# A fused hash-attention and two-layer MoE kernel: the instruction order with and without the timeline scheduler

## Chip, cores and metric

The kernel runs on one core of one Trainium2 chip. The metric is the device time of one execution in microseconds (us), lower is better. The inputs are fixed, and one launch computes everything.

## The reference

`q`, `k`, `v` have 2 batches, 8 heads, 768 positions and a head size of 64. Each query and key gets a 6-bit bucket from the signs of its product with `proj`; a query attends only to keys of its own bucket. Two dense layers with activations follow (the batch and positions make 1536 tokens, the heads a model width of 512, the inner width is 2048).

```python
q_bits = (np.einsum('bhsd,dk->bhsk', q, proj) > 0)
k_bits = (np.einsum('bhsd,dk->bhsk', k, proj) > 0)
mask = q_bucket[:, :, :, None] == k_bucket[:, :, None, :]
scores = np.where(mask, scale * np.matmul(q, k.transpose(0, 1, 3, 2)), -1000000000.0)
attn = softmax(scores)
x = np.matmul(attn, v)                    # to (tokens, 512)
h = x @ w_in1;  x = (h * sigmoid(h)) @ w_out1
h = x @ w_in2;  out = (h - np.tanh(h)) @ w_out2
```

## The kernel before, in words

**Attention.** The work is cut into 96 tiles: 16 heads (8 of each batch) of 6 blocks of 128 queries. Tile i goes through `scores` (line 243, four matmuls of TensorE into a PSUM tile `ps`), `soft_max` (line 256, VectorE: the masked row maximum and a copy into `p`), `soft_exp` (lines 264 and 265, ScalarE: a bias and the exponential), a transposition of the probabilities into `pt`, and `pv` (lines 311 to 313, 18 small matmuls with `pt` as weights). There are two ways to transpose. Every odd tile of batch 0 is turned on TensorE (`turn_p`, line 278) and split on ScalarE and VectorE (lines 280 and 281). All other tiles are split into a high half (`soft_hi`, line 290, ScalarE) and a low half (`soft_lo`, line 297, GpSimd), and a transposing DMA from SyncE's queue (line 299) fills `pt`. `pt` has four buffers. The bucket bits of a head are computed by `hash_mm` (line 172 on TensorE, line 185 on VectorE into `hb`) and copied by two DMAs of ScalarE's queue into rows of `q2` and `k2`; the second two of the four matmuls of `scores` read them. `v` of a batch is split once into `v16` and `v16l` (lines 232 and 233, six instructions each); `pv` needs both.

**The dense layers.** `Moe` runs three passes over the two layers: pass 0 is layer one for batch 0 (it runs beside the attention of batch 1), pass 1 is layer one for batch 1, and pass 2 is layer two for everything. A pass is made of groups of 12 matmuls into one PSUM bank: `h_group` (line 530) and `o_group` (line 554), eight of each per chunk of the inner width in passes 0 and 1. Weights come in pieces of 128 rows: a load (line 466 or 470), a few VectorE and ScalarE steps (lines 506 to 510, 497, 498) and a GpSimd step (line 499, or 485 for a piece read back from scratch memory). All groups of a chunk need the chunk's four pieces of their matrix.

**What sets the order.** The source is a software pipeline written by hand. One step s of `attention` emits, for several tiles at once:

```python
scores(i); soft_hi(i1); turn_p(i2); norm(...)      # i1 = i - 1, i2 = i - 2
yield s, 0
soft_max(i); pv(j); soft_lo(i2)                    # j = i - LAG, LAG = 6
yield s, 1
soft_exp(i); denom(...); split_a / split_b; load_qk
yield s, 2
```

At each `yield` the main part of the kernel puts in one piece of a step of `Moe`, on average one group of 12 matmuls per attention step. An engine runs its own instructions in the order of its list and waits at its head. Before, the list of each engine is not the source's order: when the `TileContext` closes (line 729), a scheduler plays the program on a model of time, and hands each engine its instructions in the order in which they became ready there. It weighs priorities too: `early` (line 92) raises those of the work on `v`, and `keep_in_program_order` (lines 465 and 505) pins some loads behind what stands before them.

## Time and profile before

| what | us |
|---|---|
| runs without the profiler | 795.64, 794.8, 789.62; median 794.8 |
| profiled execution, own time | 791.22 |
| profiled execution, span from first to last instruction | 789.4 |
| busy in that span: TensorE matmuls, VectorE, ScalarE, GpSimd | 733.6, 544.4, 433.1, 309.5 |

The span falls into two parts. Up to about 384 us attention and pass 0 run, with all engines and the DMA queues at work. From there to the end passes 1 and 2 run. Tile numbers below count from 0 to 95 in the source's order; "S62" would be the scores of tile 62.

### The profile page before, as it was taken

The numbers are of one execution on the slowest core, as the hardware profiler recorded it, in microseconds if no ns is written. First come the engines' busy times: TensorE is split into PE (matmuls) and PEld (weight loads), VectorE is DVE, ScalarE is ACT, GpSimd is POOL, SyncE is SP. The second block draws the span as 40 slices with busy tenths as digits, with TensorE's granted clock in tenths as the row PEclk, the third lists the DMA queues.
The fourth block names the chain that finished last, engine by engine and source line by source line (L and its number), as shares of the span: only waits on it lengthen the run. The fifth ranks groups of instructions, "written<-read, shape, count | busy, mean of one in ns | idle before, by whom it ended". The sixth has DMA issues, their size and how long they took to land.

```text
span 789.4 us, 14334 instructions
## 1 busy us (share of the span) xinstructions
PE 733.6 (93%) x5492; PEld 700.0 (89%) x5492; DVE 544.4 (69%) x1029; ACT 433.1 (55%) x821; POOL 309.5 (39%) x214
## 2 busy tenths in 40 slices
PE   4778798789989899999999999999999999999998
PEld 3667677679978798899999999999999999999998
DVE  6968688798878778778542443998768576584342
ACT  4849788797788678667443441553524334242130
POOL 4536537466777667566455420222111110110000
PEclk8899899899999999999999999999999999999999
DMA  7695776969999899994333320323112121210102
GB/s 255 190 148 106 126 154 167 212 155 197 263 245 211 214 180 240 215 218 136 97 104 107 95 81 1 101 90 130 53 56 78 57 81 33 75 54 0 52 29 81
DMA packets 138879, 100.39 MB, mean 127 GB/s; under 512 B 115870, under 2 KB 118174, under 8 KB 138810
## 3 DMA queue, kind: packets, MB, share of 16 engines
q1 hardware_dynamic: 137712, 97.54, 50.6%
q10 hardware_dynamic: 1098, 1.94, 1.0%
q8 instruction: 43, 0.70, 0.3%
q14 instruction: 26, 0.21, 0.1%
HBM read 57.95 MB, written 11.53 MB: 88 GB/s over the span
## 4 chain that ended last, share of the span: by engine, by line
PE 55%; DMA 2%; ACT 1%; DVE 0%; issue 0%; POOL 0%; ACTq 0%; DVEq 0%
PE psm L554 28%; PE psm L530 26%; DMA pt<-hl 1%; DMA w<-wi 1%; PE ps L243 0%; ACT xh L577 0%; ACT p L265 0%; POOL hl L297 0%; PE pso L311 0%; POOL wl L485 0%; ACT wh L484 0%; ACT th L536 0%; PE pso L312 0%; PE pso L313 0%; ACT hl L290 0%
## 5 line engine op out<-in xcount | busy, mean ns | idle before, releaser
L499 POOL TENSOR_TENSOR wl<-wa,wh 128x512 fp32r<-128x512 f32 x64 | 83.8, 1309 | 244.3 <-ACT wh L498 244.3
L530 PE MATMUL psm<-xh,wh 128*128 128x384 f32 x512 | 173.2, 339 | 1.6 <-ACT wh L484 1.6
L554 PE MATMUL psm<-gh,wh 128*128 128x384 f32 x512 | 173.0, 338 | 0.6 <-ACT x L346 0.4
L554 PE MATMUL psm<-gl,wh 128*128 128x384 f32 x512 | 171.5, 335 | 0.0
L530 PE MATMUL psm<-xl,wh 128*128 128x384 f32 x512 | 171.4, 335 | 0.0
L530 PE MATMUL psm<-xh,wl 128*128 128x384 f32 x512 | 170.0, 335 | 0.0
L554 PE MATMUL psm<-gh,wl 128*128 128x384 f32 x512 | 169.4, 335 | 0.0
L297 POOL TENSOR_TENSOR hl<-p,hl 128x768 f16<-128x768 f32 x72 | 120.4, 1674 | 88.0 <-ACT hl L290 82.5
L256 DVE TENSOR_SCALAR_CACHE_REDUCE p<-ps 128x768 f32<-128x768 f32 x96 | 90.8, 952 | 29.7 <-PE ps L243 20.0
L530 PEld LDWEIGHTS psm<-xh,wh 128*128 128x128 f32 x512 | 96.5, 188 | 2.1 <-ACT wh L484 1.9
L243 PE MATMUL ps<-k,q 128*128 128x384 f32 x336 | 82.9, 372 | 15.9 <-DVE p L256 9.0
L554 PEld LDWEIGHTS psm<-gh,wh 128*128 128x128 f32 x512 | 96.3, 188 | 1.5 <-ACT x L346 0.6
L554 PEld LDWEIGHTS psm<-gl,wh 128*128 128x128 f32 x512 | 96.4, 188 | 0.0
L530 PEld LDWEIGHTS psm<-xl,wh 128*128 128x128 f32 x512 | 96.4, 188 | 0.0
L566 DVE TENSOR_TENSOR acc<-acc,psm 128x384 f32<-128x384 f32 x96 | 52.1, 551 | 63.5 <-PE psm L554 63.1
L530 PEld LDWEIGHTS psm<-xh,wl 128*128 128x128 f32 x512 | 95.9, 188 | 0.0
L554 PEld LDWEIGHTS psm<-gh,wl 128*128 128x128 f32 x512 | 95.8, 188 | 0.0
L542 DVE TENSOR_TENSOR gl<-psm,gh 128x384 fp32r<-128x384 f32 x128 | 70.6, 554 | 31.9 <-ACT gh L541 31.7
L265 ACT ACTIVATE p<-p,bi 128x768 f32<-128x768 f32 x96 | 89.0, 939 | 2.9
L541 ACT CAST gh<-psm 128x384 fp32r<-128x384 f32 x128 | 61.4, 480 | 50.5 <-DVE psm L540 35.1
L311 PE MATMUL pso<-v,pt 128*128 128x65 f16 x576 | 70.9, 200 | 15.4 <-DMA pt<-hl 15.3
L311 PEld LDWEIGHTS <-pt 128*128 128x128 f16 x576 | 55.3, 101 | 27.2 <-DMA pt<-hl 17.4
(90 smaller groups left out, 1267.2 us busy)
## 6 DMA issues: line engine op xcount, KB each, us to landing
w<-in_w_in_dram SPq DMA_DIRECT2D x32, 512.0 KB
w<-in_w_out_dram SPq DMA_DIRECT2D x32, 512.0 KB
r<-in_qkT_dram SPq DMA_DIRECT2D x15, 768.0 KB
wi<-wa SPq DMA_DIRECT2D x16, 256.0 KB
wo<-wa SPq DMA_DIRECT2D x16, 256.0 KB
w<-wi SPq DMA_DIRECT2D x16, 256.0 KB
w<-wo SPq DMA_DIRECT2D x16, 256.0 KB
vr<-in_v_dram SPq DMA_DIRECT2D x6, 512.0 KB
```

The source lines that it names most:

```text
L243: nc.tensor.matmul(out=ps[:, u, 0:HS], lhsT=a[:, t * 128:(t + 1) * 128], rhs=c[:, u * HS:(u + 1) * HS], start=(j == 0), stop=(j == 1))
L256: nc.vector.tensor_scalar(p.rearrange("p (c s) -> p c s", c=2), pss.pop(i)[:, :, 0:HS], FLOOR, None, op0=ALU.max, op1=ALU.max, accum_out=m)
L265: nc.scalar.activation(out=p, in_=p, func=ACTF.Exp, scale=0.125, bias=bi)
L297: nc.gpsimd.tensor_tensor(hl[:, 1, :], p, hl[:, 0, :], op=ALU.subtract)
L311: nc.tensor.matmul(out=o, lhsT=pt[:, kt, :], rhs=v16[:, kt, h, :], start=(kt == 0), stop=False)
L499: nc.gpsimd.tensor_tensor(ll, s, hh.bitcast(F32), op=ALU.subtract)
L530: nc.tensor.matmul(out=ps, lhsT=a[:, k, fs], rhs=b_[blk][:, k, :], start=(k == 0 and j == 0), stop=(k == KD - 1 and j == 2))
L541: nc.scalar.copy(gh[:, f, :], ps)
L542: nc.vector.tensor_tensor(gl[:, f, :], ps, gh[:, f, :].bitcast(F32), op=ALU.subtract)
L554: nc.tensor.matmul(out=ps, lhsT=a[:, f, ds], rhs=b_[:, f, :], start=(f == 0 and j == 0), stop=(f == F - 1 and j == 2))
L566: nc.vector.tensor_tensor(ac, ac, ps, op=ALU.add)
```

## The change

The change is one argument. With it, the lists are made without the model of time.

```diff
-    with _tile.TileContext(nc, schedule_with_timeline_sim=True) as tc:
+    with _tile.TileContext(nc, schedule_with_timeline_sim=False) as tc:
         lsh_attention_moe_kernel(tc, *args)
```

No instruction is added or removed; the same 7220 of TensorE, 935 of VectorE, 855 of ScalarE, 219 of GpSimd and 241 of SyncE stand in other places. The mean move is 15 places on TensorE, 2.4 on VectorE, 3.4 on ScalarE and under 1 on GpSimd and SyncE. The new lists are close to the order of the source and not equal to it: going down VectorE's list, the next instruction is an earlier one of the source 273 times before and 247 times now.

The first place is VectorE's list in batch 0, around the bucket bits of head 5 (`hb_1255`, line 185), which the scores of tiles 30 to 35 read. `ps_1349` and `ps_1396` are the scores of tiles 24 and 25, `pt_1187` is the turned tile 21. Before:

```order
L281 TENSOR_TENSOR pt_1097<-psm_1098,pt_1097 128x384
L256 TENSOR_SCALAR p_1369,mx_1370<-ps_1349 128x768
L256 TENSOR_SCALAR p_1402,mx_1403<-ps_1396 128x768
L256 TENSOR_SCALAR p_1458,mx_1459<-ps_1438 128x768
L281 TENSOR_TENSOR pt_1097<-psm_1104,pt_1097 128x384
L256 TENSOR_SCALAR p_1497,mx_1498<-ps_1492 128x768
L281 TENSOR_TENSOR pt_1187<-psm_1188,pt_1187 128x384
L185 TENSOR_SCALAR hb_1255<-psm_1256,cst_sb_69 82x384
L281 TENSOR_TENSOR pt_1187<-psm_1194,pt_1187 128x384
L185 TENSOR_SCALAR hb_1255<-psm_1257,cst_sb_69 82x384
```

Now:

```order
L281 TENSOR_TENSOR pt_1097<-psm_1098,pt_1097 128x384
L256 TENSOR_SCALAR p_1289,mx_1290<-ps_1269 128x768
L281 TENSOR_TENSOR pt_1097<-psm_1104,pt_1097 128x384
L256 TENSOR_SCALAR p_1322,mx_1323<-ps_1317 128x768
L281 TENSOR_TENSOR pt_1187<-psm_1188,pt_1187 128x384
L281 TENSOR_TENSOR pt_1187<-psm_1194,pt_1187 128x384
L185 TENSOR_SCALAR hb_1255<-psm_1256,cst_sb_69 82x384
L185 TENSOR_SCALAR hb_1255<-psm_1257,cst_sb_69 82x384
L256 TENSOR_SCALAR p_1369,mx_1370<-ps_1349 128x768
```

The bits were made after four maxima that now stand behind them, and the two halves of each item are no longer set among others.

The second place is TensorE's list in batch 1, around the scores of tile 62 (`ps_3163`). `pt_3012` is the transposed tile 57, `pt_2952` is tile 56, and `psm_3149` is a group of pass 0. Before:

```order
L311 LDWEIGHTS pt_3012
L311 MATMUL pso_3058<-v16_2444,pt_3012 128x65
L243 MATMUL ps_3163<-k1_2713,q1_2711 128x384 x2
L243 MATMUL ps_3163<-k2_2714,q2_2712 128x384 x2
L312 LDWEIGHTS pt_3012
L312 MATMUL pso_3058<-v16l_2445,pt_3012 128x65
```

Now:

```order
L554 MATMUL psm_3149<-gl_2397,wh_2411 128x384
L554 MATMUL psm_3149<-gh_2396,wl_2412 128x384
L243 MATMUL ps_3163<-k1_2713,q1_2711 128x384 x2
L243 MATMUL ps_3163<-k2_2714,q2_2712 128x384 x2
L311 LDWEIGHTS pt_2952
L311 MATMUL pso_3058<-v16_2444,pt_2952 128x65
```

Before, the scores stood inside the `pv` of the tile five behind; now they stand between a whole group of 12 and the whole `pv` of the tile six behind.

The third place is TensorE's list at the end of pass 0. `psm_5563`, `psm_5587`, `psm_5607` are three of its last eight groups of line 554, all of which need the pass's last weight piece for their last three matmuls; `psm_5543` is its last group of line 530. Before:

```order
L554 MATMUL psm_5607<-gl_5263,wh_5280 128x384
L554 MATMUL psm_5607<-gh_5262,wl_5281 128x384
L554 MATMUL psm_5563<-gh_5262,wh_5280 128x384
L554 MATMUL psm_5563<-gl_5263,wh_5280 128x384
L554 MATMUL psm_5587<-gh_5262,wh_5280 128x384
L554 MATMUL psm_5587<-gl_5263,wh_5280 128x384
```

Now:

```order
L530 MATMUL psm_5543<-xh1_71,wl_4833 128x384
L554 MATMUL psm_5563<-gh_5262,wh_5280 128x384
L554 MATMUL psm_5563<-gl_5263,wh_5280 128x384
L554 MATMUL psm_5563<-gh_5262,wl_5281 128x384
L554 MATMUL psm_5563<-gh_5262,wh_5280 128x384
L554 MATMUL psm_5563<-gl_5263,wh_5280 128x384
```

The three groups were begun one after the other and finished together, with matmuls of pass 1 set among them; now the first is written out with all its 12 before the next goes on, and pass 1 begins behind the last.

## Rows read from the trace of the kernel before

**Rows 1.** The page, part 2: TensorE's busy tenths and granted clock in 40 slices
```profile
PE   4778798789989899999999999999999999999998
...
PEclk8899899899999999999999999999999999999999
```

**Rows 2.** Windows: busy us of PE, PEld, DVE, ACT, POOL, then clock, DMA share, GB/s
```profile
0.00:50.00 50.00, 30.23 (x217) 25.67 (x218) 37.99 (x75) 31.22 (x54) 24.20 (x19) 0.86 0.80 203
50.00:190.00 140.00, 118.11 (x1334) 103.87 (x1334) 113.68 (x229) 111.89 (x217) 77.05 (x48) 0.93 0.72 158
190.00:350.00 160.00, 151.89 (x1379) 139.31 (x1378) 127.51 (x250) 120.11 (x210) 107.39 (x69) 0.99 1.03 222
350.00:384.00 34.00, 31.56 (x251) 29.61 (x250) 23.07 (x44) 21.48 (x47) 21.31 (x18) 1.00 0.55 147
384.00:789.40 405.40, 401.84 (x2319) 401.52 (x2317) 242.11 (x435) 148.41 (x297) 79.53 (x61) 1.00 0.21 68
```

**Rows 3.** The chain that ended last: start us, us, what; the first of 23 such
```profile
403.12 16.64 PE psm L554 x96
```

**Rows 4.** Waits of PE from 10 to 190 us: total us, times, longest
```profile
PE ps L243 <- DVE p L256: 9.0, 10, 2.9
PE pso L311 <- DMA pt<-hl: 8.3, 3, 3.9
PE ps L243 <- DMA k<-hb: 5.4, 4, 3.3
PE ps L243 <- DMA l<-hb: 4.0, 2, 3.5
PE pso L312 <- DVE v16l L233: 3.6, 2, 2.2
```

**Rows 5.** Waits of PE from 190 to 350 us
```profile
PE pso L311 <- DMA pt<-hl: 6.5, 5, 2.7
PE ps L243 <- DVE p L256: 1.4, 3, 0.9
```

**Rows 6.** Timeline of DVE near 25 us: start us, us, instruction
```profile
23.29 0.80 DVE L233 SCALAR_TENSOR_TENSOR v16l<-vr,vsc,v 128x512 f16<-128x512 f32 x1
...
26.43 3.62 DVE L233 SCALAR_TENSOR_TENSOR v16l<-vr,vsc,v 128x512 f16<-128x512 f32 x3
```

**Rows 7.** Lines by shape: count, then busy us, mean ns of one, idle before
```profile
L297 POOL TENSOR_TENSOR hl<-p,hl 128x768 f16<-128x768 f32 x72 | 120.4, 1674 | 88.0 <-ACT hl L290 82.5 <-DMA k<-hb 3.9 <-DVE p L256 0.7
...
L256 DVE TENSOR_SCALAR_CACHE_REDUCE p<-ps 128x768 f32<-128x768 f32 x96 | 90.8, 952 | 29.7 <-PE ps L243 20.0 <-PE psm L278 5.8 <-POOL wl L499 1.7
L265 ACT ACTIVATE p<-p,bi 128x768 f32<-128x768 f32 x96 | 89.0, 939 | 2.9
...
L290 ACT CAST hl<-p 128x768 f16<-128x768 f32 x72 | 59.9, 833 | 4.8 <-DVE cv L510 1.8 <-DMA q<-hb 1.0 <-ACT p L265 0.7
...
L233 DVE SCALAR_TENSOR_TENSOR v16l<-vr,vsc,v 128x512 f16<-128x512 f32 x12 | 14.7, 1241 | 0.1
```

**Rows 8.** The chain again: two transposing DMAs from issue to release
```profile
322.84 5.53 DMA pt<-hl
...
351.86 4.80 DMA pt<-hl
```

**Rows 9.** Windows for line 256 alone: its instructions on DVE in batch 0
```profile
50.00:130.00 80.00, 31.15 (x66) 0.94 0.64 133
```

**Rows 10.** Timeline of POOL: the last weight piece of pass 0
```profile
374.60 1.28 POOL L499 TENSOR_TENSOR wl<-wa,wh 128x512 fp32r<-128x512 f32 x1
```

**Rows 11.** Timeline of PE: the last matmul of line 530 in pass 0
```profile
368.52 0.33 PE L530 MATMUL psm<-xh,wl 128*128 128x384 f32 x1
```

**Rows 12.** The chain: the last 36 matmuls of line 554 in pass 0
```profile
383.71 6.24 PE psm L554 x36
```

**Rows 13.** Windows around a wait of TensorE at 85 us
```profile
85.00:90.00 5.00, 1.55 (x7) 1.34 (x7) 0.79 (x2) 2.69 (x6) 4.25 (x3) 0.69 1.02 142
90.00:95.00 5.00, 5.00 (x57) 4.88 (x56) 2.07 (x5) 3.81 (x8) 2.06 (x2) 0.63 0.07 14
```

## Prediction

> **What bounds the kernel now.** I read the page's slices first. TensorE is busy nine tenths or more in every slice from the middle on, and never quite full before it; its clock is whole late and falls to 8 or 9 tenths in the early slices [rows 1]. Then the windows, which cut the span by stage [rows 2]. From 384 us to the end TensorE is busy 401.8 of 405.4 us. The chain that ended last says the same: from 403 us on it is nothing but packets of 96 matmuls, each 16.64 us long, 0.173 us for a matmul, with no wait between them (23 such rows) [rows 3]. That stretch is bound by TensorE alone, and no order of the same matmuls can shorten it.
>
> So the whole question lies in the first 384 us. TensorE is idle there for 50 - 30.2 = 19.8 us in the start, 140 - 118.1 = 21.9 us in the attention of batch 0 and the change of batches, 160 - 151.9 = 8.1 us in batch 1, and 34 - 31.6 = 2.4 us in the end of pass 0, together 52.2 us [rows 2]. No other engine is full either: in the 140 us of batch 0 VectorE is busy 113.7 and ScalarE 111.9, some 80% [rows 2]. That is the picture of engines that wait for one another at the head of their lists, which is what the change touches. The waits of TensorE say for what [rows 4, 5]: until 190 us for the row maximum that frees the scores' PSUM (9.0 us), for the transposing DMA that fills `pt` (8.3), for the DMAs of the bucket bits (5.4 + 4.0), and for `v16l` (3.6); in batch 1 almost only for `pt` (6.5 of 8.1).
>
> **The change part by part.** The sum is made against the profiled execution's own 791.2 us (span 789.4 and 1.8 around it). That is 3.6 us under the median of the runs, 794.8, and inside their scatter. Nothing is added or removed, so every term is a wait that goes, comes or moves.
>
> *Passes 1 and 2.* TensorE's list is group after group in both, and what prepares weights has whole groups to hide under. 0 us; the idle time there, 3.6 us, bounds a gain, and I allow as much for a loss.
>
> *Bucket bits.* Before, VectorE makes the bits of head 5 after the maximum of tile 27, and the scores of tile 30 need them. Now they come before that of tile 24. The same holds for heads 2, 6 and 7, by 2 to 4 tiles; heads 3 and 4 come 1 and 2 tiles later, which still leaves them over a tile ahead of their use. Of the 9.4 us of waits for the bits, about 3.3 belong to head 1 in the start, and 6.1 to later heads [rows 4]. These go: -6 us (0 to -9). What is late next is the maximum of the tile before, a wait that the same rows show at 0.9 us a time.
>
> *Start.* The six instructions that make `v16l` stood one to three at a time between the maxima of tiles 3 to 7; now all six stand ahead of the maximum of tile 3, and a half of head 1's bits behind it. One such instruction took 0.80 us, three in a row 3.62 [rows 6], and the group's mean is 1.24 [rows 7]: six are 4.8 to 7.4 us of delay for the maxima of tiles 3 to 6. Behind them stand the exponentials, and TensorE, which has `pv` of tiles 0 and 1 to do in the meantime. The maxima are not VectorE's last word here, since it waits for bits anyway at tile 6. I take +4 (0 to +7).
>
> *Transposed tiles in batch 0.* Counted in the lists, a tile's `pv` stood on average 7.8 tiles behind the newest scores before and stands 6.4 behind now; in the middle of the batch it was 9 to 12 and is 6 to 9. The new list also sets three or four `pv` in a row. A tile that goes through the DMA needs, after its maximum, an exponential (0.94), a cast (0.83), the low half (1.67) [rows 7] and the DMA (4.8 to 5.5) [rows 8], 8.2 to 9.0 us. The pace of this stage is 80 us for 33 maxima (each has two records), 2.4 us a tile [rows 9], so a lead of 6 tiles is 14.5 us and most fit, but the DMA can only start once the `pv` four tiles back has freed a buffer. In a row of four the last one then waits for its own DMA. I take +4 (-8, if all 8.3 us of rows 4 go, to +19 with the first rival).
>
> *Change of batches.* TensorE waited 3.6 us for `v16l` of batch 1 [rows 4]. Its six instructions were set among the maxima of tiles 52 to 54 and now stand in one block between the maxima of tiles 50 and 51, 4.8 to 7.4 us long as above, while `pv` of tile 48 stands before the next groups of pass 0. Those groups start earlier too, because their first weight pieces are ready 3 to 6 tiles earlier. +1 (-4 to +6).
>
> *Batch 1.* Here the lead grows, from 3.8 tiles on average to 5.1 and to a steady 6 in the middle, where a step is scores, one whole `pv`, one whole group. One step is at least 4 + 12 matmuls of 0.173 us, 2.8 us, and `pv`; two more steps of slack are 6 us, more than the longest wait for `pt`, 2.7 us [rows 5]. The 6.5 us go. In their place, a step's maximum must now be done within the group between two scores; the wait for it, 1.4 us in all [rows 5], may double. -5 (-8 to +8: VectorE is busy 127.5 of 160 us [rows 2] and a regular step gives it less freedom).
>
> *End of pass 0.* The last groups of line 554 need the last weight piece. GpSimd ended it at 374.60 + 1.28 = 375.9 us [rows 10], when TensorE had begun the last matmul of line 530 at 368.5 [rows 11]. Before, it bridged the 7.4 us with pieces of four groups and with matmuls of pass 1, 20 of them up to the end of the pass. Now the first group alone gives it 9 matmuls, 1.6 us, and it waits some 5.6; the 84 matmuls left of that line take 14.6 us, to 390.5. Before, the same line ended at 383.71 + 6.24 = 389.9 [rows 12] with 20 x 0.173 = 3.5 us of pass 1 done besides. So +4 (0 to +6).
>
> Sum: 0 - 6 + 4 + 4 + 1 - 5 + 4 = +2, on 791.2, which is 793. That lies between the profiled execution and the median, so I forecast no difference that can be measured: for this kernel about 1% is what a measurement can tell from none. All lower ends together are 33 us under the start of the sum, all upper ends 49 over it, so 35 below and 47 above its result; the terms do not reach their ends at once, and a third of the way to either gives 782 to 808 as this case's own range.
>
> **The clock.** After TensorE had been busy only 1.55 of 5 us, its granted clock was 0.69 and then 0.63 in a stretch where it was busy throughout [rows 13]; of its two levels, 1.2 and 2.4 GHz, that is a mixture with much of the lower one. The Trainium skill (TensorE: Matmul & The Clock Gate, "HAM oscillation — how this bites in real kernels") says that an engine which keeps falling idle between bursts goes back to the half clock each time; the trace agrees, 0.63. By that rule the first rival below would cost more than its waits: 5.0 us of work at 0.63 instead of whole is 1.9 us, seven times 13, an estimate of 821. By the windows the mean clock of that stage is 0.93 [rows 2] and TensorE has idle time to spare there, so neither the sum nor the rival's price has it.
>
> **Rivals.**
>
> *Rows of `pv` wait (slower).* In batch 0 the new list has about seven places with three or four `pv` in a row ahead of the next scores. If in each the last DMA is late, the scores behind it are late, then the maximum, and every engine with them, because TensorE can't take the scores first. The price is that of such a wait now, 8.3 / 3 = 2.8 us [rows 4]: 7 x 2.8 = 19 instead of 4, so 793 + 15 = 808. For it speaks that the row before shows exactly this wait, up to 3.9 us; against it that the 6 tiles are 14.5 us. It decides from where a DMA takes more than about 7 us to land: it has to share the queue with loads of `q` and `k`.
>
> *One step fits the next (faster).* If the regular order lets VectorE and ScalarE run on in batch 0 as well, half of the 21.9 us of idle TensorE goes [rows 2], the price of `pt` (+4) does not come up, and the end of pass 0 is covered: 793 - 11 - 4 = 778. The even 80% of both engines speaks for it; against it, the waits then have to shrink everywhere at once.
>
> *The new order is hardly another.* The lists still are a scheduler's, and VectorE's moves are 2.4 places. Then all terms shrink together and the time stays at 791 to 795.
>
> **How the numbers follow.** I give the summed case 0.45 (within 1% in 0.29 of it, faster in 0.07, slower in 0.09), the rows of `pv` 0.27, nearly all slower, the good fit 0.20, all faster, and the last 0.08. Faster by over 1%: 0.07 + 0.20 = 0.27. Slower: 0.09 + 0.25 = 0.34. Within 1%: 0.39, the rest. The range reaches beyond both priced rivals: 774 to 816.
>
> **What would show it right or wrong.** After the change, the waits for bucket bits should be gone except for head 1; TensorE's waits for `pt` should be near none between the batches' change and the end of pass 0, and larger before; about 5 us of wait should stand inside the first group of line 554 behind the last of line 530; and from there to the end the windows should be as now. It is wrong if the passes after pass 0 show waits, or if the maximum of a tile becomes TensorE's main wait in batch 1.

## The result, and the profile after

| | before | after |
|---|---|---|
| 20 runs without the profiler, median | 790.77 us (784.37 to 799.68) | 797.07 us (792.54 to 799.98) |
| ratio, 95% interval | | 1.0075 (1.0055 to 1.0094) |
| profiled execution, own time | 791.22 us | 794.17 us |
| its span | 789.4 us | 792.4 us |

The change makes the kernel slower by about 6 us, 0.75%: less than the 1% that I took as the bound, but clear of zero. The prediction, 793.0, is 4.1 us under the median. The trace shows 1.2 of that: its execution is 2.95 us over the old one, at 794.17, where my sum had +2. The other 2.9 us are scatter, since this execution lies that far under the median of its own kernel. So the two traces show about half of the 6.3 us between the medians, and the windows below place only that half. That the sum comes so near is luck: its small error hides larger ones, as the windows show.

The page's slices of the changed kernel, as in [rows 1]:

```profile
PE   4688876788989999999999999999999999999998
```

From the middle on TensorE is as full as before. In the first half it is one tenth fuller in slices 3 and 5 and two tenths emptier in slices 6 and 7, from 99 to 139 us. The windows of [rows 2] for the changed kernel (the same columns):

```profile
0.00:50.00 50.00, 31.95 (x245) 27.12 (x246) 37.91 (x78) 30.55 (x53) 19.80 (x17) 0.86 0.71 208
50.00:190.00 140.00, 112.71 (x1268) 98.31 (x1268) 109.31 (x222) 108.92 (x210) 75.82 (x48) 0.94 0.70 149
190.00:350.00 160.00, 150.97 (x1405) 140.56 (x1401) 129.60 (x256) 125.15 (x223) 112.45 (x73) 0.99 1.05 230
350.00:384.00 34.00, 31.23 (x253) 29.60 (x250) 23.40 (x42) 19.06 (x41) 20.03 (x18) 1.00 0.59 147
384.00:792.40 408.40, 405.00 (x2337) 404.68 (x2335) 242.32 (x433) 147.79 (x297) 77.77 (x60) 1.00 0.22 67
```

TensorE's idle time (length less busy) is 18.1 us in the start, where it was 19.8; 27.3 where it was 21.9; 9.0 where it was 8.1; 2.8 where it was 2.4; and 3.4 after 384 us, where it was 3.6. So the loss lies in the second window. Its waits from 10 to 190 us, and then from 190 to 350 us, beside [rows 4, 5]:

```profile
PE ps L243 <- DVE p L256: 9.5, 12, 2.1
PE pso L311 <- DMA pt<-hl: 8.2, 6, 3.1
PE pso L311 <- DVE xt L329: 4.7, 3, 3.0
...
PE pso L312 <- DVE v16l L233: 0.8, 1, 0.8
...
PE ps L243 <- DMA k<-hb: 0.8, 1, 0.8
```

```profile
PE psm L554 <- POOL wl L499: 2.8, 1, 2.8
PE ps L243 <- DVE p L256: 2.5, 2, 1.4
PE ps L243 <- DMA k<-hb: 1.3, 1, 1.3
...
PE pso L311 <- DMA pt<-hl: 0.7, 1, 0.7
```

The waits that I expected to go are gone: those for bucket bits (9.4 us, now 0.8 and 1.3), for `v16l` (3.6, now 0.8), and for `pt` in batch 1 (6.5, now 0.7). In their place stand waits that the old trace has none of: for the normalisation on line 329, for the exponential on line 265 (5.4 us, most of it before 95 us), and for a weight piece on line 499. The wait for head 0's own bits (line 181), right at the start, grew from 1.3 to 3.9 us. Finer windows say where. Before:

```profile
50.00:100.00 50.00, 42.58 (x487) 36.16 (x487) 34.60 (x75) 39.02 (x77) 27.29 (x16) 0.93 0.61 125
100.00:135.00 35.00, 29.59 (x362) 25.66 (x361) 31.87 (x66) 29.44 (x60) 18.91 (x12) 0.95 0.70 151
135.00:165.00 30.00, 24.54 (x300) 22.12 (x297) 23.09 (x52) 22.30 (x42) 15.01 (x12) 0.89 0.90 212
165.00:195.00 30.00, 26.39 (x228) 24.58 (x226) 29.11 (x51) 24.78 (x47) 19.53 (x12) 0.94 0.78 179
195.00:265.00 70.00, 64.11 (x592) 57.77 (x592) 53.90 (x105) 54.46 (x96) 50.92 (x33) 0.98 1.06 237
```

After:

```profile
50.00:100.00 50.00, 43.36 (x560) 37.27 (x560) 37.13 (x83) 41.20 (x80) 30.39 (x18) 1.00 0.64 136
100.00:135.00 35.00, 23.79 (x239) 19.82 (x238) 30.95 (x56) 25.86 (x52) 16.32 (x12) 0.89 0.74 158
135.00:165.00 30.00, 24.90 (x307) 22.49 (x307) 21.03 (x46) 22.74 (x44) 15.57 (x11) 0.90 0.74 151
165.00:195.00 30.00, 24.71 (x211) 22.16 (x210) 23.79 (x47) 23.07 (x45) 18.29 (x12) 0.94 0.75 158
195.00:265.00 70.00, 63.77 (x551) 59.18 (x550) 54.65 (x108) 55.51 (x99) 49.26 (x32) 0.98 1.04 235
```

Up to 100 us the new order is ahead by 2.5 us of TensorE's busy time. In the 35 us from 100 to 135 it loses 5.8 (29.59 to 23.79); some 2 us of such a figure are scatter, as e13 will show. Two places turned out to matter.

**The first place: the first four weight pieces.** ScalarE, VectorE and TensorE of the changed kernel near 110 us:

```profile
109.31 0.66 ACT L506 ACTIVATE wa<-w 128x512 f32<-128x512 f32 x1 [2.73 <-DMA w<-in_w_in_dram]
```

```profile
110.01 0.43 DVE L507 TENSOR_SCALAR wa<-wa 128x512 f32<-128x512 f32 x1 [2.63 <-ACT wa L506]
110.35 0.55 DVE L329 TENSOR_TENSOR xt<-pso,den 128x384 f32<-128x384 f32 x1
```

```profile
110.95 0.21 PE L311 MATMUL pso<-v,pt 128*128 128x65 f16 x1 [3.02 <-DVE xt L329]
```

ScalarE stands 2.73 us at the head of its list for the load of the first piece. VectorE's step for that piece stands ahead of the normalisation of head 4, so it waits 2.63 us for ScalarE, and the first `pv` of the next head, which needs the normalised head out of its PSUM bank, holds TensorE for 3.02 us. One load, issued by SyncE only at 104.77 us, stops three engines. Three more pieces follow in the same way among the maxima of tiles 36 to 44, where VectorE is busy 30.95 of 35 us.

**The second place: GpSimd near 256 us.** Its timeline, and what TensorE did:

```profile
254.18 1.85 POOL L159 TENSOR_TENSOR q<-r,q 64x768 fp32r<-64x768 f32 x1
256.11 1.81 POOL L163 TENSOR_TENSOR k<-r,k 128x768 fp32r<-128x768 f32 x1
257.87 1.26 POOL L499 TENSOR_TENSOR wl<-wa,wh 128x512 fp32r<-128x512 f32 x1
```

```profile
259.19 0.44 PE L554 MATMUL psm<-gh,wl 128*128 128x384 f32 x1 [2.80 <-POOL wl L499]
```

The step of line 499 makes the low half of piece 15 (counted from 0), the last that the second chunk's groups of line 554 need. ScalarE had ended its part at 254.5 us, but two steps for head 13, 1.85 and 1.81 us long, stood ahead of it in GpSimd's list. TensorE waits 2.80 us at its head, and VectorE and ScalarE behind it 3.3 and 3.0.

### The profile page after: what moved, and what is told of

It reads as the page before. It is cut to its first block, busy times and chain, and to the rows that moved or that the text cites. A ratio compares the mean times of both kernels' runs of the same rounds, so it can differ in the third digit from the quotient of the medians.

```text
span 792.4 us, 14317 instructions
## 1 busy us (share of the span) xinstructions
PE 731.9 (92%) x5492; PEld 700.3 (88%) x5492; DVE 542.5 (68%) x1029; ACT 431.5 (54%) x821; POOL 305.9 (39%) x214
## 4 chain that ended last, share of the span: by engine, by line
PE 55%; POOL 0%; ACT 0%; issue 0%; DVE 0%; POOLq 0%; ACTq 0%
PE psm L530 27%; PE psm L554 27%; POOL wl L499 0%; PE pso L311 0%; ACT p L265 0%; PE pso L312 0%; PE pso L313 0%; POOL xl L578 0%; ACT hl L290 0%; DVE acc L566 0%; POOL hl L297 0%; ACT th L536 0%; ACT x L346 0%; ACT gh L541 0%; PE psm L334 0%
## 5 line engine op out<-in xcount | busy, mean ns | idle before, releaser
L554 PE MATMUL psm<-gh,wl 128*128 128x384 f32 x512 | 171.8, 336 | 3.1 <-POOL wl L499 3.1
L530 PE MATMUL psm<-xh,wl 128*128 128x384 f32 x512 | 172.1, 336 | 2.0 <-POOL wl L499 2.0
L311 PE MATMUL pso<-v,pt 128*128 128x65 f16 x576 | 68.2, 200 | 16.6 <-DMA pt<-hl 8.9
L243 PEld LDWEIGHTS ps<-k,q 128*128 128x128 f32 x336 | 61.1, 201 | 22.2 <-DVE p L256 12.5
```

The costliest lines, as they stand in the source:

```text
L243: nc.tensor.matmul(out=ps[:, u, 0:HS], lhsT=a[:, t * 128:(t + 1) * 128], rhs=c[:, u * HS:(u + 1) * HS], start=(j == 0), stop=(j == 1))
L311: nc.tensor.matmul(out=o, lhsT=pt[:, kt, :], rhs=v16[:, kt, h, :], start=(kt == 0), stop=False)
L530: nc.tensor.matmul(out=ps, lhsT=a[:, k, fs], rhs=b_[blk][:, k, :], start=(k == 0 and j == 0), stop=(k == KD - 1 and j == 2))
L554: nc.tensor.matmul(out=ps, lhsT=a[:, f, ds], rhs=b_[:, f, :], start=(f == 0 and j == 0), stop=(f == F - 1 and j == 2))
```

## The experiments

My first theory (A in the texts on record) put the loss into the first place. All runs were timed against the old kernel; each had the timeline scheduler off unless said otherwise. "Ratio" is to the old kernel, whose median was 790.5 to 792.6 us beside them.

**Half of each order (e1 to e3, and the control e8).** The lists of both kernels were read out, and an edge that sets order alone, without a wait, was put from each instruction to the next of the wanted list. What the source writes up to a cut follows one order, the rest the other.

```diff
         lsh_attention_moe_kernel(tc, *args)
+        pin_order(tc, nc)
...
+        for a, b in zip(seq, seq[1:]):
+            tc.add_manual_dep(b, a.name, dep, reason="pin_order")
```

> The new order on every engine for all that the source writes before the scores of tile 48, the old order for the rest. Theory A (the loss is made in batch 0, from tile 33 on, where ScalarE and VectorE wait at the heads of their lists for the first weight pieces of pass 0): 795 to 799 us, as slow as the whole change. Theory B (the loss is made later: groups of the dense layer are held back in batch 1 and at the end of pass 0): 789 to 792.

> The other half: the old order up to the scores of tile 48, the new one from there to the end. Theory A: 786 to 791 us, since the new order gains some 3 us in batch 1 where the waits for pt go. Theory B: 794 to 798.

> The new order only for what the source writes before the step that begins the weights of pass 0 (tile 32), the old order for the rest. Theory A: 788 to 792 us, nothing lost, perhaps some gained, since the trace of the new order is up to 6 us ahead at tiles 12 to 24. Theory C (the start and the rows of pv lose, as my first rival had it): 794 to 798.

Measured: 805.33 us, ratio 1.0197 (1.0154 to 1.0241); 804.14, 1.0172 (1.0134 to 1.0209); 797.16, 1.0096 (1.0061 to 1.0130). The first two miss both theories: each half of the change is slower than the whole. The third fits theory C, but has a cut too. Hence a control, the old order in both halves with the cut between:

> The control for the two runs that put half of each order together: the old order in both halves, but with everything that the source writes before the scores of tile 48 ahead of everything after it, on every engine. If the cut itself made both halves slow: 799 to 804. If it costs nothing, 789 to 792, and then the two orders must disturb one another.

Measured: 801.01, ratio 1.0103 (1.0071 to 1.0135). The cut alone costs 1%, I take it because the old order carries work of one side far into the other; that is not tested. Taken off, the halves cost 0.9% and 0.7%, together more than the 0.75% of the whole, at the edge of what the intervals allow. These runs do not place the loss.

**ScalarE behind VectorE (e4, e5, e7).** From 95 to 190 us ScalarE waited 7.2 us at line 498 for VectorE's last step on a piece (line 497), and 5.9 us at line 506 for loads; before it was 1.3 and 0.5. The edit issues the first two loads 3 steps ahead and puts the two lines a yield apart:

```diff
-            if s == half - PRE and sub == 0:
+            if s == half - PRE - 3 and sub == 0:
                 moe.begin()
+            if s == half - PRE and sub == 0:
                 pre = moe.first_weights()
...
             def last():
-                nc.vector.scalar_tensor_tensor(r, lo, 29, u, op0=ALU.logical_shift_right, op1=ALU.bitwise_or)
                 nc.scalar.copy(hh, s)
...
+                lambda: nc.vector.scalar_tensor_tensor(r, lo, 29, u, op0=ALU.logical_shift_right,
+                                                       op1=ALU.bitwise_or),
                 last,
```

> The changed kernel, with the first two weight loads issued 3 steps ahead of their first use and the step of line 497 put one yield ahead of that of line 498, so that ScalarE no longer stands waiting for VectorE's last step on the same piece. Theory A: ScalarE's waits at these two lines from 95 to 190 us fall from 13 us to under 6, and the time falls by 3 to 5 us, to 792 to 794. Rival (these waits lie beside TensorE's other waits): they fall as much and the time stays at 796 to 798.

Measured: 789.29, ratio 0.9990 (0.9964 to 1.0016), 8 us under the changed kernel; ScalarE's waits fell to 6.0. Only the second half of the edit:

> One half of the edit of the run before alone: the step of line 497 one yield ahead of that of line 498, the loads left where they are. If ScalarE's waiting behind VectorE's last step on a piece is what cost, this half brings most of the 8 us back: 789 to 793. If it was the loads that ScalarE waited for, the time stays at 795 to 798.

Measured: 792.18, ratio 1.0002 (0.9975 to 1.0030). The first is 3 us faster than its range, the second inside its own, and together they looked like the answer. But the trace put the gain elsewhere. From 100 to 135 us TensorE was hardly better, 24.50 us busy; it was better from 195 to 265:

```profile
195.00:265.00 70.00, 67.24 (x602) 63.13 (x602) 57.45 (x115) 56.62 (x100) 50.11 (x32) 0.97 1.02 219
```

That is 3.5 us more than the 63.77 of the changed kernel. And the edit had also moved GpSimd's list there. Of GpSimd, in the changed kernel and then in e5 (`wl_3327` is the matrix of which piece 15 is a part, line 498 of e5 is line 499 of the others, `q2_3820` and `k1_3821` are head 13):

```
L297 TENSOR_TENSOR hl_3732<-p_3682,hl_3732 128x768
L159 TENSOR_TENSOR q2_3820<-r_3655,q1_3819 64x768
L163 TENSOR_TENSOR k1_3821<-r_3655,k2_3822 128x768
L499 TENSOR_TENSOR wl_3327<-wa_3540,wh_3326 128x512
```

```
L159 TENSOR_TENSOR q2_3820<-r_3655,q1_3819 64x768
L498 TENSOR_TENSOR wl_3327<-wa_3540,wh_3326 128x512
L297 TENSOR_TENSOR hl_3732<-p_3682,hl_3732 128x768
L163 TENSOR_TENSOR k1_3821<-r_3655,k2_3822 128x768
```

With the timeline scheduler on, both edits together:

> Both edits of e4_pieces_spread with the timeline scheduler on. If the model of time already kept ScalarE from standing behind VectorE (its trace has 1.3 us of this wait where the new order has 7.2), there is little to win: 788 to 792. Rival, that the edit is a gain by itself whatever the order: 782 to 786.

Measured: 794.44, ratio 1.0034 (1.0004 to 1.0063), 2 us over the range given: the edit is no gain by itself.

**GpSimd's one place (e13).** To part the two readings, only piece 15 was moved:

```diff
...
+    for op in qk_low[13]:
+        tc.add_manual_dep(op.ins, low[15].ins.name,
+                          mybir.DependencyInfo(mybir.DependencyClass.NoSync, mybir.DependencyReason.DATA),
+                          reason="piece first")
```

> The changed kernel with one move: on GpSimd, the low half of piece 15 (the last that line 554's first groups of the second chunk need) stands ahead of the two steps for head 13 of 1.9 us each, instead of behind them. All other lists stay, but for one matmul of TensorE. If this place alone is what the second chunk's first groups waited for (TensorE 2.8 us, VectorE 3.3 and ScalarE 3.0 behind it): TensorE busy 66.5 or more of the 70 us from 195 to 265 (63.8 in the changed kernel), and 790 to 794 us. Rival (the gain of e5_split_step came from ScalarE no longer standing behind VectorE): 795 to 798 us.

Measured: 792.92, ratio 1.0022 (0.9989 to 1.0054), 4 us under the changed kernel, and

```profile
195.00:265.00 70.00, 67.40 (x611) 62.79 (x611) 59.15 (x117) 57.62 (x104) 52.31 (x34) 1.00 1.05 237
```

ScalarE still waits behind VectorE in it, from 95 to 190 us:

```profile
ACT wh L499 <- DVE wa L498: 7.3, 6, 3.1
```

That is what it was in the changed kernel, 7.2. So ScalarE's standing is not needed to explain the gain, and GpSimd's order at piece 15 is what makes it: one instruction two places earlier on an engine that is busy 70% of batch 1. The other traces agree. Wherever piece 15 stands ahead of both steps or of the second (e4, e5, e9, e10 and e13 to e17), TensorE is busy 66.5 to 68.6 us from 195 to 265; where it stands behind both (the changed kernel, e2, e11 and e12), 63.4 to 64.6.

**The place of the first four pieces (e6, e12, e10, e11).** One number in the source sets at which step they begin:

```diff
-PRE = 28
+PRE = 23
```

> The changed kernel with PRE = 23 instead of 28: the first four weight pieces enter the lists 5 steps later, about where the old order had them, so some 11 us of VectorE's work move from tiles 36 to 44 into tiles 41 to 49 and the change of batches. If the place of these pieces is what makes TensorE lose 5.8 us between 100 and 135 us: 791 to 794, and TensorE busy 27 to 30 of those 35 us. Rival: the pieces are then late for the first groups of the dense layer and the loss only moves to 165 to 195 us: 796 to 800.

> The same kernel as e6_weights_5_steps_later, whose trace was taken in a disturbed execution. Theory: 787 to 793 us, and TensorE busy 27 to 30 us of the 35 between 100 and 135 us, where it was busy 29.6 in the old order and 23.8 in the new; ScalarE's waits for line 497 and for the loads there under 5 us.

Measured: 790.06, ratio 0.9990 (0.9967 to 1.0013); the second, a single run taken for its trace, 788.93. From 100 to 135 us, in that trace:

```profile
100.00:135.00 35.00, 27.50 (x350) 24.38 (x348) 30.99 (x59) 28.62 (x57) 20.36 (x12) 0.95 0.78 155
```

3.7 of the 5.8 us are back, as expected. But this figure scatters: e13, whose lists are those of the changed kernel on every engine up to 254 us, has 25.83 us there in place of 23.79, and e14 below, with the lists of PRE = 23, has 26.45. Firmer is how far VectorE has come. Its 46th maximum, of tile 45, in the changed kernel and then with PRE = 23:

```profile
137.35 0.94 DVE L256 TENSOR_SCALAR_CACHE_REDUCE p<-ps 128x768 f32<-128x768 f32 x1
```

```profile
129.71 0.94 DVE L256 TENSOR_SCALAR_CACHE_REDUCE p<-ps 128x768 f32<-128x768 f32 x1
```

In e13 it begins at 135.59 and in e14 at 128.22, so the two orders are 7 us apart there and the scatter is under 2; at the 58th maximum it is still 4 to 5 us. From 95 to 140 us ScalarE no longer waits for these loads (3.2 us in the changed kernel, none here), and TensorE's waits for line 329 fall from 4.3 to 1.5 us. Then 33 and 18:

> PRE = 33 instead of 28 in the changed kernel: the four pieces now stand among the maxima of tiles 31 to 38, where VectorE has as little time to spare as in tiles 36 to 44, and the change of batches has none of this work. If what counts is how much of it lies in the busy batch 0 and how little in the change of batches: 796 to 800, no better than the changed kernel. If it was the collision with head 7's and head 8's bits and norms just there: 789 to 793.

> PRE = 18: the pieces stand among the maxima of tiles 46 to 49 and in the change of batches. If VectorE's time in batch 0 is what counts, it is all free of them now: 786 to 791, as long as the first groups do not wait. If the first groups need the pieces by then: 793 to 800, with TensorE's waits for the last GpSimd step of a piece before tile 52.

Measured for 33: 793.86, ratio 1.0034 (1.0008 to 1.0059), between what the two theories said. Its trace has the loss earlier, and no loss at the second place, because its GpSimd list is there as in e5:

```profile
50.00:100.00 50.00, 40.37 (x509) 34.13 (x508) 36.72 (x81) 37.48 (x75) 26.06 (x16) 1.00 0.70 149
100.00:135.00 35.00, 25.51 (x274) 21.37 (x274) 32.25 (x57) 26.29 (x53) 19.55 (x13) 0.90 0.66 153
...
195.00:265.00 70.00, 67.50 (x579) 63.42 (x580) 56.21 (x113) 55.29 (x99) 48.36 (x31) 0.94 1.00 225
```

From 50 to 135 us TensorE is idle 19.1 us here, 17.9 in the changed kernel (85 less 43.36 and 23.79) and 12.8 in the old: batch 0 pays for these pieces wherever in it they stand. Measured for 18: 792.71, ratio 1.0006 (0.9985 to 1.0027), again between the two. Batch 0 is free of them, the change of batches pays, and the second place is as in the changed kernel (64.21 us from 195 to 265):

```profile
100.00:135.00 35.00, 27.67 (x370) 23.83 (x368) 26.52 (x57) 29.44 (x61) 18.01 (x11) 0.99 0.56 98
135.00:165.00 30.00, 22.72 (x178) 19.52 (x178) 25.73 (x47) 21.54 (x39) 19.11 (x15) 0.67 0.85 222
```

**Both places (e9, e14), and two controls.**

> The changed kernel with both edits of e4_pieces_spread and PRE = 23. If the place of the first four pieces in the list and ScalarE's standing behind VectorE are two separate costs, they add: 7 us from each against the changed kernel's 797, to 782 to 786, under both kernels. If they are one cost, met in two ways, the time stays at 787 to 791.

> The same move together with PRE = 23. If the two places are the whole loss and independent: 783 to 788 us, as fast as e9_later_and_spread, which had the split step and the early loads besides. Rival (the split step or the early loads have a gain of their own): 788 to 791, no better than PRE = 23 alone.

Measured: 786.56, ratio 0.9946 (0.9911 to 0.9981), between the range for two costs that add and that for one; and 784.97, ratio 0.9898 (0.9853 to 0.9944). The last is the fastest kernel of the study, 1.0% under the old one by the ratio and 0.8% by the medians: PRE = 23 and piece 15 first on GpSimd, and nothing else. It needs neither the split step nor the early loads. From 195 to 265 us:

```profile
195.00:265.00 70.00, 68.12 (x629) 63.24 (x628) 59.38 (x118) 56.16 (x101) 53.08 (x34) 1.00 1.03 236
```

Whether later weights help any order:

> The old order (timeline scheduler on) with PRE = 23. If the gain of PRE = 23 belongs to the place that the new order gives these pieces: 789 to 794, nothing gained, since the old order already puts them 3 to 6 tiles later. Rival (later weights are better under any order): 782 to 787.

Measured: 800.99, ratio 1.0113 (1.0069 to 1.0157), slower than both ranges. Later weights cost the old order 1%; it already had these pieces later. So the gain belongs to the place that the new order gave them. Whether the waits for `pt` that remain are due to its four buffers:

> e9_later_and_spread with LAG = 5. pt has four buffers, and with a lag of 6 the DMA of a tile has to wait for a pv that is written only four steps later. If that is what TensorE's 12 us of waits for pt there are: 780 to 785 us. Rival (the shorter lag takes away more time than the buffer gives): 788 to 795.

Measured: 790.02, ratio 0.9983 (0.9958 to 1.0009), against 0.9946 without it. TensorE's waits for `pt` from 10 to 350 us are 12.1 us there, 11.7 in e9: a shorter lag does not take them away.

**The bucket bits (e15, e17).** Order edges hold the bits of heads 2, 5, 6 and 7 back behind the maxima after which the old order had them (for head 2, its first half):

```diff
...
+    for n, i in ((2, 10), (5, 26), (6, 32), (7, 38)):
+        for u in range(2):
+            tc.add_manual_dep(bits[n, u].ins, tops[i].ins.name,
...
```

> The changed kernel with the bucket bits of heads 2, 5, 6 and 7 held back behind the maxima of tiles 10, 26, 32 and 38, as the old order had them. If the waits for the bits were worth the 6 us of my term: 800 to 805 us, with TensorE's waits for the bits' DMAs back at 5 us or more from 10 to 190 us. Rival (the wait is only exchanged for another in a stage that VectorE and ScalarE set): 795 to 799, with these waits back but others gone.

> e14_later_piece_first with the bucket bits of heads 2, 5, 6 and 7 held back as in e15_bits_as_before; here GpSimd's place of piece 15 is the same in both. If the bits' place is worth my term of 6 us: 789 to 793. If it is worth nothing in this order: 783 to 787, as e14.

Measured: 791.74, ratio 0.9994 (0.9961 to 1.0028), and 796.00, ratio 1.0062 (1.0034 to 1.0090). The first misses both ranges, on the fast side; its GpSimd list had moved at piece 15 as in e5, so it is to be set beside e5, 1.0002, or e13, 1.0022, and then the bits' place is worth nothing. Both ranges also had the waits for the bits' DMAs back; in its trace TensorE has none from 10 to 190 us. So it was not the earlier place of these bits that took the waits away. The second run, where piece 15's place is kept, is 11 us slower than e14. The edges moved much else in its lists, on every engine from 50 us on, so the 11 us are not the bits' alone. One wait of its trace is for bits, at head 8, whose VectorE steps end 3.7 us later than in e14:

```profile
151.53 0.66 PE L245 MATMUL ps<-k,q 128*128 128x384 f32 x1 [4.56 <-DMA k<-hb]
```

That is less than half of the 11 us. From 190 to 350 us TensorE is idle 4.0 us longer than in e14 (9.7 and 5.7), and why is open. So holding the bits back costs nothing in one surrounding, and in another, with all that it moves, 1.7%.

## Why the prediction was right or wrong

*Passes 1 and 2, 0 us.* Right: idle 3.4 us there, 3.6 before.

*Bucket bits, -6 us.* The waits went (9.4 to 2.1 us), but the mechanism is not shown: in e15 the bits are late again and the waits stay away. Nor is the price: 0 by e15 beside e5, while e17 beside e14, 11 us, moves much else.

*Start, +4 us.* Right in its place, wrong as a sum. The scores of tile 6 began 4.7 us later (29.75 us, before 25.02), and the six instructions of line 233 took 4.45 us in a row, a little under what I had costed. But by 50 us TensorE had done more than before, 31.95 against 30.23 us busy at the same granted clock, and the 13th maximum began at 50.63 us, before 55.80.

*Transposed tiles in batch 0, +4 us.* Too much: the waits for `pt` are 8.2 us, before 8.3, and the longest 3.1. The rows of three and four `pv` fit, so the first rival did not come.

*The step that failed* is in the term on the change of batches: "Those groups start earlier too, because their first weight pieces are ready 3 to 6 tiles earlier." I read the move as a gain and gave it no cost in the stage it moved into. The moved work was not counted: 16 steps of VectorE, and the waits of ScalarE and VectorE for loads and for each other. Batch 0 lost by it: TensorE's busy time fell by 5.8 us from 100 to 135, and PRE = 23 gives back 0.8% of the whole (1.0075 to 0.9990), some 7 us. How the 7 us divide between the steps, the loads and the blocking told of below, no run separates. I had read that VectorE is busy 80% of this stage [rows 2], which left the moved steps little cover. The term itself, +1, fits the idle time from 135 to 195 us, 9.1 before and 10.4 after.

*Batch 1, -5 us.* Half right: the waits for `pt` fell by 5.8 us. What is late next was named wrongly. I named the maximum of a tile (1.4 to 2.5 us); it was GpSimd's piece 15. So idle time there rose by 0.9 us where I had it fall by 5, and e13 returns 0.5%.

*End of pass 0, +4 us.* Wrong in its mechanism: no wait of 5 us stands there. The last matmul of line 530 began at 372.60 us, before 368.52, and GpSimd ended the last piece at 375.07, so TensorE had 0.28 us to wait for it:

```profile
375.12 0.44 PE L554 MATMUL psm<-gh,wl 128*128 128x384 f32 x1 [0.28 <-POOL wl L499]
```

Put together: the waits whose end I forecast (bits, `v16l`, `pt` in batch 1) were gone, and two losses that I had not seen took more than that gave. With both places mended, the new order is 1% faster than the old one (e14), about half of the way from the 791.2 of the sum to the second rival's 778. (That rival's own sum takes off only one of the two +4 that it names; with both it is 774.) The two places add, as far as the noise tells: against the changed kernel's median e13 gains 4.2 us, e6 7.0 and e14 12.1; by the ratios it is 0.5%, 0.8% and 1.8%, where the four intervals together leave some 0.6% open, by my estimate. What stays open is the price of the halves e1 and e2, and of the bits.

## What to carry to other kernels

A move that makes something ready earlier puts its work, and its engines' waits for the load, among what stands there now: cost it in that stage, against the engine that is fullest there. When waits at one releaser go, look at the last member of every set that a later group needs all of, on every engine with long steps in its list, also those far from full. And an experiment on order needs its control: an edit meant for one engine moved another engine's list here, and the gain came with that; a cut between two orders cost 1% by itself.

## What the runs showed of the hardware

The same VectorE step took up to three times as long where GpSimd was at work. VectorE's steps on the first pieces in the changed kernel (start, us), and GpSimd's beside them:

```profile
113.51 2.04 DVE L497 SCALAR_TENSOR_TENSOR wa<-w,wa 128x512 int32<-128x512 int32 x1
...
116.73 1.10 DVE L508 TENSOR_SCALAR wa<-wa 128x512 int32<-128x512 int32 x1
...
124.66 0.42 DVE L508 TENSOR_SCALAR wa<-wa 128x512 int32<-128x512 int32 x1
125.47 1.67 DVE L510 SCALAR_TENSOR_TENSOR wa<-w,wa 128x512 int32<-128x512 int32 x1
127.53 0.68 DVE L497 SCALAR_TENSOR_TENSOR wa<-w,wa 128x512 int32<-128x512 int32 x1
```

```profile
113.34 1.66 POOL L297 TENSOR_TENSOR hl<-p,hl 128x768 f16<-128x768 f32 x1 [7.73 <-ACT hl L290]
116.27 1.28 POOL L499 TENSOR_TENSOR wl<-wa,wh 128x512 fp32r<-128x512 f32 x1 [1.28 <-ACT wh L498]
...
124.86 1.73 POOL L297 TENSOR_TENSOR hl<-p,hl 128x768 f16<-128x768 f32 x1 [1.27 <-issue]
```

Line 497 took 0.68 us alone and 2.04 when it began beside GpSimd's step that ended at 115.00; the rest of that step, 1.49, and 0.68 make 2.17. For line 508 it is 0.82 and 0.42, 1.24, measured 1.10; for line 510 1.12 and 0.68, 1.80, measured 1.67 (0.68 as it took alone at 118.63). So each seems to wait for GpSimd's step to end and then to run whole. The Trainium skill (SBUF — State Buffer, "Who interferes with whom") says so: a VectorE instruction with two inputs in SBUF, or in a mode that uses both its ports, shares a port pair with GpSimd, and the one that comes second is fully blocked. The trace agrees to 0.14 us. Line 508 has one input, and whether it runs in such a mode no trace here shows. The four pieces took VectorE 16.3 us in the changed order and 13.0 in the old (the four lines' busy time). With PRE = 23 it is 14.7 us (e12) and 15.0 (e14), so this is at most 1.6 us of what the first place costs. From the fifth piece on one input lies in PSUM, and line 497 takes 0.68 us on average:

```profile
L497 DVE SCALAR_TENSOR_TENSOR wa<-w,cv 128x512 int32<-128x512 int32 x60 | 40.8, 680 | 1.2
...
L497 DVE SCALAR_TENSOR_TENSOR wa<-w,wa 128x512 int32<-128x512 int32 x4 | 6.0, 1498 | 0.0
```

The clock scatters too. Up to 50 us the lists of the changed kernel and of e13 are the same, and TensorE is busy 31.95 us at a granted clock of 0.86 in the one trace (above) and 30.80 us at 0.97, nearer to 2.4 GHz throughout, in the other, for the same 245 matmuls:

```profile
0.00:50.00 50.00, 30.80 (x245) 25.38 (x245) 36.94 (x77) 30.50 (x54) 19.73 (x17) 0.97 0.76 204
```

That is 1.2 us of TensorE's busy time with no cause in the program. It is no time of the kernel's: the 13th maximum began at 50.63 us in the one trace and at 51.01 in the other. So a window's busy time is to be read with its clock beside it.
